# Retention, ELU block and gated block on one core: odd head pairs' outputs on the other half of the partitions, inputs in gated quarters, x stored as 2 KB rows

## The chip, the core and the metric

The kernel runs on one core of a Trainium2 chip. Its time is the device time of one execution in microseconds. Before the change the median of three runs is 872.62 us (871.51 to 873.28). The one execution that was profiled took 868.8 us, with a span of 867.0 us between its first and last instruction.

## What is computed

Three stages follow each other; all arrays are float32.

```python
# q, k, v: (4, 8, 576, 64): batch, heads, positions, head size
scores = (q @ k.T) / 8
ret = scores * D          # D[i, j] = gamma_h ** (i - j) for i >= j, else 0
x = (ret @ v) put as (2304 tokens, 512 = 8 heads * 64)
h = x @ w_in              # 512 -> 2048
y = elu(h) @ w_out        # 2048 -> 512
out = (sigmoid(y @ w_gate) * (y @ w_val)) @ w_out2    # 512 -> 1536 -> 512
```

## The kernel before, in words

**Retention** is done in 18 steps (class `Step`, `NSTEP`). A step n takes 128 positions of one batch (the last step of each half of the batches takes 64 positions of two). The eight heads are four pairs p; a pair is 128 partitions, head h = 0 on partitions 0 to 63 and h = 1 on 64 to 127. A step cuts its 128 positions into two halves X of 64. All its matmuls (L274, helper `mm`) are 64 by 64, so that one uses a quarter of TensorE's array: which half of the rows it takes is set by the partitions of what it reads, which half of the columns by the partitions of what it writes.

- `scores` (L276) fills the PSUM tile `ts`; `causal` (L283, VectorE) masks it into `a`.
- `sums` (L289) and `states` (L299) make the running state of each head in the other PSUM tile `to` and in `st`.
- `inter` (L318) multiplies the state with q: rows of half h, output (method `o`, L315) on the partitions of half h. It goes twice over pairs and heads: first with X = 1 - h, then with X = h. Steps with c = 0 (n = 0, 1, 9, 10) have a state for X = 1 only and issue half of these matmuls.
- Between its two halves `inter` puts a `nop` on SyncE (on GpSimd in step 1) that waits for the first half. `outs` (L330), which adds the part within a half (rows of half X, output on half h), starts with a wait for this `nop`. It is needed because row halves change the place that they add to.
- `x_mul` (L342, VectorE) scales the result by `cq_sb` into `xf`; `x_high` and `x_low` split it into two parts for the next matmuls, and `x_low` stores `xf` to memory (L365) in `whole[g]`, one tile [128, KB, 512] for 512 tokens, so that one step's 128 tokens are rows of 512 B.

**The feed-forward part.** `ff` is a list of units; unit s of the main loop (L1089) makes one block of 128 hidden values for 256 tokens (512 from s = 18 on): `ups` (L385, matmuls at L380), ELU, a split into `g`, and `downs` of unit s - 2 (L421, matmuls at L114 to L116). Up to s = 15 it also calls `block(s + 2)`, the retention step n = s + 2: `inter(n)`, `scores(n + 1)`, `outs(n)`, `sums(n + 1)`, then the VectorE part, the loads and the store. From s = 4 on the block stands ahead of the unit's `ups`, before that behind it. Each engine runs its instructions in the order in which they are written here.

**Loads.** All loads are issued by SyncE, in order. `Step.load` brings a step's 1 MB of q, k and v; from step 9 (`FIRST_APART`) in two parts, the second kept in the list `rest` until `begin_rest(f)` issues it behind the end of unit f's matmuls (after `ups` and after `downs`). Weights are loaded by `Weight.load` (512 KB, rows of 4 KB) and then made from 64-bit to two 32-bit parts by `Weight.chain` (ACT, VectorE, GpSimd), in a scratch tile t chosen by a number in L185. Those of w_in are `weights[0]`, `[2]`, `[4]`, `[6]` and so on; the main loop loads `weights[4]`, `[5]`, `[6]`, `[7]` and `W["i", 4]` behind the `downs` in s = 4, 7, 10, 13 and 11 (L1158). A DMA's completion is told by one of eight semaphores, which the DMAs of SyncE and ACT take in turn; a DMA that takes a semaphore whose last DMA hasn't landed waits for it on its engine.

**Later parts.** From s = 18 on the stored x is read back twice: `prep` (L1061) reads tokens 0 to 1023 in four transfers of 512 KB; `reload` (L989) reads tokens 1024 to 2047 in two of 1 MB. The rest of the ELU block and the gated block use a two by two scheme with seven products of blocks (`unit`, L518; products in the order 1, 7, 6, 2, 5, 3, 4). Converted weights are kept in memory and brought back by `restore` (L1048). In the last unit of the ELU block (`q + 1 == QN`, L1302) the gated block's first weights ("v", 0), ("g", 0) and ("s", 0) are restored.

```python
                    for n, i in zip(back[-1:] + back[:-1], (0, 2, 4, 6, 8)):
                        plan[i] = [*plan[i], lambda n=n: restore(n)]
```

Of the kernel before, what the change touches and what calls it, by code (L numbers as in the profile page):

```python
# [11 lines left out]
F32 = mybir.dt.float32  # L12
BF16 = mybir.dt.bfloat16
F32R = mybir.dt.float32r
I32 = mybir.dt.int32
# [6 lines left out]
NP = H // 2  # L22
# [6 lines left out]
HC = 64  # L29
# [25 lines left out]
def retention_elu_glu(  # L55
# [81 lines left out]
    class Weight:  # L137
        def __init__(self, src, slot, at=None, home=w_tile):
            self.src, self.slot, self.at, self.home, self.w = src, slot, at, home, None

        def load(self, raw=None):
            self.ours = raw is None
            self.raw = raw_free.popleft() if self.ours else raw
            return sp.dma_start(out=self.raw, in_=self.src.bitcast(I32))

# [36 lines left out]
    for f in range(FA):  # L182
        for n, src in (("i", w_in), ("o", w_out)):
            i = len(weights)
            W[n, f] = Weight(src[f], i % 8, (0, 0, 1, 1, 0, 1, 0, 1)[i] if i < 8 else t_slot(n, f))  # L185
            weights.append(W[n, f])
# [39 lines left out]
    class Step:  # L226
# [16 lines left out]
        def load(self):  # L243
            if self.n in SPARE:
                self.t = spare_y[SPARE[self.n]].rearrange("p (q c) -> p q c", q=NP)
            else:
                self.t = inpool.tile([128, NP, 4 * C], F32, tag="in", name="in")
            self.q, self.kT, self.k, self.v = (self.t[:, :, i * C : i * C + C] for i in range(4))
            if self.last:
                self.load_half(0)  # L250
            elif self.n < FIRST_APART:
                sp.dma_start(out=self.t, in_=ain[self.b, self.c].rearrange("p r x -> r p x"))
            else:
                self.load_pairs(0)
                rest.append(lambda: self.load_pairs(1))

        def load_pairs(self, i):
            p = slice(2 * i, 2 * i + 2)
            return sp.dma_start(out=self.t[:, p, :], in_=ain[self.b, self.c][p].rearrange("p r x -> r p x"))

# [53 lines left out]

        def o(self, h, X, p):  # L315
            return to[64 * h : 64 * h + 64, X, 256 + HC * p : 256 + HC * p + HC]

        def inter(self):  # L318

            for other in (1, 0):  # L320
                for p in range(NP):
                    for h in range(2):
                        X, r = h ^ other, slice(64 * h, 64 * h + 64)
                        if X or self.c:
                            ins = self.mm(self.o(h, X, p), self.st[X][r, p, :], self.q[r, p, HC * X : HC * X + HC], p == 0)
                if other:

                    self.swept = after((pool if self.n == 1 else sp).nop(), ins)

        def outs(self):  # L330

            for p in range(NP):
                for h in range(2):
                    for X in range(2):
                        r = slice(64 * X, 64 * X + 64)
                        ins = self.mm(self.o(h, X, p), self.v[r, p, 64 * h : 64 * h + 64], self.a[r, h, p, :],
                                      not self.c and not X and p == 0)
                        if self.swept:
                            after(ins, self.swept)
                            self.swept = None  # L340

# [18 lines left out]
        def x_low(self):  # L360
            dve.tensor_tensor(out=self.x[1], in0=self.xf, in1=self.x[0].bitcast(F32), op=ALU.subtract)
            if self.g < 4:
                if not self.at:
                    whole[self.g] = dpool.tile([128, KB, 512], F32, tag=f"x{self.g}", name="x")
                sp.dma_start(out=whole[self.g][:, :, self.at : self.at + 128], in_=self.xf)  # L365

# [435 lines left out]
    with tc.manual_schedule():  # L802
# [32 lines left out]
        for X in range(2):  # L835
            r = slice(64 * X, 64 * X + 64)
            act.dma_start(out=tri[r], in_=csmall[r, 5 * NP + 64 * X : 5 * NP + 64 * X + HC])
        act.dma_start(out=cq_sb, in_=cq)
        for X in range(2):
# [18 lines left out]

        def begin_rest(f):
            while rest:  # L860
                after(rest.pop(0)(), f.end)

        def block(n, scales=True):

            more = n + 1 < NSTEP
            steps[n].inter()
            if more:
                steps[n + 1].scores()
            steps[n].outs()
# [47 lines left out]
        warm_up(3)  # L917
        steps[1].inter()
        steps[1].outs()
# [61 lines left out]
        def close():  # L981
            raw_shut[:] = more_raws
            for r in more_raws:
                for i, o in enumerate(raw_free):
                    if o is r:
                        del raw_free[i]
                        break

        def reload(to):  # L989
            for g in (2, 3):  # L990
                to[g] = y_tile(g)
                sp.dma_start(out=to[g], in_=whole[g].rearrange("p k t -> p (k t)"))

# [67 lines left out]
        def prep():  # L1061
# [3 lines left out]

            def source(g, k):
                return whole[g][:, k * KH : k * KH + KH, :].rearrange("p k t -> p (k t)")

            def sum(name):
# [3 lines left out]
            for name, (g, k) in {"11": (0, 0), "12": (1, 0), "22": (1, 1), "21": (0, 1)}.items():  # L1073
                sp.dma_start(out=f[name], in_=source(g, k))
            for _ in range(8):
# [13 lines left out]
        for s in range(end):  # L1089
# [23 lines left out]
            if s == 0:  # L1113
                def middle():
                    stages(w2, 1)
                    steps[2].scores()
                    steps[2].sums(True)
# [13 lines left out]
            if s == 1:  # L1131
# [3 lines left out]
                warm_up(WARM[4])  # L1135
                steps[3].inter()
                steps[4].scores()
                steps[3].outs()
# [126 lines left out]
        for pair in (first, second):  # L1265
# [3 lines left out]
            for q in range(Q0, QN):  # L1269
# [19 lines left out]
                else:  # L1289
# [12 lines left out]
                    else:  # L1302
                        back += [("v", 0), ("g", 0), ("s", 0)]
                    for n, i in zip(back[-1:] + back[:-1], (0, 2, 4, 6, 8)):
                        plan[i] = [*plan[i], lambda n=n: restore(n)]
# [175 lines left out]
```

## Time and profile before

| | before |
|---|---|
| median of 3 runs | 872.62 us |
| profiled execution | 868.8 us, span 867.0 us |
| PE | 852.4 us busy, 98% |
| DVE | 664.7 us, 77% |
| ACT | 459.3 us, 53% |
| POOL | 409.4 us, 47% |
| DMA | 194.83 MB, mean 225 GB/s |
| TensorE clock | 0.997 of full speed |
| issue to landing, median: input loads of 512 KB | 5.3 us |
| w_out loads of 512 KB | 3.6 us |
| `reload`'s two loads of 1 MB | 10.5 us |

PE is TensorE's matmuls, DVE VectorE, ACT ScalarE, POOL GpSimd, SPq SyncE's queue of instructions. A busy PE counts overlapping matmuls once, so it doesn't tell how many quarters of the array work side by side; that is read from the times at which matmuls start.

### The profile page before, as it was taken

The page shows a single profiled execution, that of the slowest core. Times are in us where ns is not written, and L with a number is a line of the kernel's source. Part 1 is how long each engine was busy: PE and PEld are TensorE (multiplying, and loading weights), DVE is VectorE, ACT ScalarE, POOL GpSimd, SP SyncE. Part 2 cuts the span into 40 slices and gives each one's busy share as a digit, 9 for nine tenths or more (in the row PEclk, how much of TensorE's full clock was granted, in tenths as well). Part 3 has the DMA queues.
Part 4 walks back from the last instruction along what each step waited for, and adds up shares of the span by engine and source line. Part 5 has one row for each costly group of instructions (what it writes and reads, how often), then busy time and mean ns, then how long its engine had stood idle before and what let it go on. Part 6 is the DMA issues. An engine that isn't in the chain of part 4 may idle for free.

```text
span 867.0 us, 16196 instructions
## 1 busy us (share of the span) xinstructions
PE 852.4 (98%) x6375; PEld 728.9 (84%) x6375; DVE 664.7 (77%) x967; ACT 459.3 (53%) x833; POOL 409.4 (47%) x327
## 2 busy tenths in 40 slices
PE   8899999999999999999999999999999999999998
PEld 5798998888888888888878888888888888888886
DVE  5867758789999888887887988589967564777775
ACT  3445475677666666666665665445543344343331
POOL 2445435656546543564552565244543244334453
PEclk9999999999999999999999999999999999999999
DMA  9978628745474696898774765646574665464322
GB/s 339 298 245 245 185 74 314 292 145 202 163 229 184 230 404 227 314 377 274 274 326 176 239 239 210 218 157 196 197 277 157 229 235 194 192 237 170 112 114 98
DMA packets 63852, 194.83 MB, mean 225 GB/s; under 512 B 9888, under 2 KB 19104, under 8 KB 57376
## 3 DMA queue, kind: packets, MB, share of 16 engines
q1 hardware_dynamic: 62512, 192.30, 61.8%
q10 hardware_dynamic: 1264, 1.49, 0.5%
q8 instruction: 50, 0.82, 0.4%
q14 instruction: 26, 0.21, 0.1%
HBM read 127.19 MB, written 66.58 MB: 223 GB/s over the span
## 4 chain that ended last, share of the span: by engine, by line
PE 88%; DVE 4%; DMA 3%; issue 2%; ACT 2%; POOL 1%; SPq 0%; ACTq 0%; DVEq 0%; POOLq 0%
PE u L114 13%; PE u L115 13%; PE u L116 13%; PE acc L114 10%; PE acc L115 10%; PE acc L116 10%; PE tile L114 3%; PE tile L115 3%; PE tile L116 3%; PE to L274 3%; PE h L380 2%; DMA w<-c 2%; PE h L114 1%; PE h L115 1%; PE h L116 1%
## 5 line engine op out<-in xcount | busy, mean ns | idle before, releaser
L110 POOL TENSOR_TENSOR g<-e,g 128x512 fp32r<-128x512 f32 x95 | 133.7, 1412 | 223.8 <-ACT g L109 196.8
L114 PE MATMUL u<-x,s 128*128 128x512 f32 x288 | 112.6, 391 | 0.0
L115 PE MATMUL u<-x,s 128*128 128x512 f32 x288 | 112.3, 390 | 0.0
L116 PE MATMUL u<-x,s 128*128 128x512 f32 x288 | 112.1, 389 | 0.0
L114 PE MATMUL u<-x,w 128*128 128x512 f32 (+1 forms) x264 | 98.3, 372 | 1.5 <-DMA w<-c 1.3
L115 PE MATMUL u<-x,w 128*128 128x512 f32 (+1 forms) x264 | 98.0, 371 | 0.0
L116 PE MATMUL u<-x,w 128*128 128x512 f32 (+1 forms) x264 | 97.7, 370 | 0.0
L109 ACT CAST g<-e 128x512 fp32r<-128x512 f32 x101 | 61.9, 620 | 65.0 <-DVE e L598 39.7
L172 POOL TENSOR_TENSOR w<-t,w 128x512 fp32r<-128x512 f32 x37 | 51.0, 1378 | 41.1 <-ACT w L169 37.5
L114 PEld LDWEIGHTS u<-x,s 128*128 128x128 f32 x288 | 54.1, 188 | 11.5 <-ACT u L522 0.7
L116 PEld LDWEIGHTS u<-x,s 128*128 128x128 f32 x288 | 54.1, 188 | 11.5
L115 PEld LDWEIGHTS u<-x,s 128*128 128x128 f32 x288 | 54.2, 188 | 10.3
L759 DVE TENSOR_TENSOR y<-y,tile 128x512 f32<-128x512 f32 x76 | 51.2, 680 | 10.8 <-PE tile L116 10.6
L114 PE MATMUL acc<-g,w 128*128 128x512 f32 (+1 forms) x168 | 58.2, 346 | 0.4 <-ACT y L440 0.4
L795 DVE TENSOR_TENSOR y<-y,acc 128x512 f32<-128x512 f32 x58 | 39.1, 682 | 25.4 <-PE acc L116 25.0
L114 PEld LDWEIGHTS u<-x,w 128*128 128x128 f32 x264 | 49.8, 189 | 10.2 <-DMA w<-c 1.7
L115 PE MATMUL acc<-g,w 128*128 128x512 f32 (+1 forms) x168 | 57.7, 344 | 0.0
L116 PE MATMUL acc<-g,w 128*128 128x512 f32 (+1 forms) x168 | 57.7, 343 | 0.0
L116 PEld LDWEIGHTS u<-x,w 128*128 128x128 f32 x264 | 49.7, 188 | 8.7
L115 PEld LDWEIGHTS u<-x,w 128*128 128x128 f32 x264 | 49.9, 189 | 7.4
L675 DVE TENSOR_TENSOR y<-y,acc 128x512 f32<-128x512 f32 (+1 forms) x68 | 39.6, 606 | 19.8 <-PE acc L116 17.9
L114 PE MATMUL acc<-w,g 128*128 128x512 f32 (+1 forms) x152 | 54.1, 356 | 0.0
(226 smaller groups left out, 2418.3 us busy)
## 6 DMA issues: line engine op xcount, KB each, us to landing
w<-c SPq DMA_DIRECT2D x72, 512.0 KB, 6.7
c<-w SPq DMA_DIRECT2D x48, 512.0 KB, 4.9
s<-c SPq DMA_DIRECT2D x22, 1024.0 KB, 7.1
c<-s SPq DMA_DIRECT2D x18, 1024.0 KB, 4.9
y<-y SPq DMA_DIRECT2D x8, 1024.0 KB, 6.2
in<-in_ain SPq DMA_DIRECT2D x6, 1024.0 KB, 8.9
raw<-in_w_in SPq DMA_DIRECT2D x12, 512.0 KB, 4.8
in<-in_ain SPq DMA_DIRECT2D x12, 512.0 KB, 5.3
```

Of the source, the lines that this page charges most:

```text
L109: act.copy(hi, src)
L110: lo_engine.tensor_tensor(out=lo, in0=src, in1=hi.bitcast(F32), op=ALU.subtract)
L114: pe.matmul(out_, wh, xh, start=start, stop=False, skip_group_check=shared)
L115: pe.matmul(out_, wh, xl, start=False, stop=False, skip_group_check=shared)
L116: return pe.matmul(out_, wl, xh, start=False, stop=stop, skip_group_check=shared)
L172: lo_engine.tensor_tensor(out=w[:, 1, :], in0=f, in1=w[:, 0, :].bitcast(F32), op=ALU.subtract)
L274: return pe.matmul(out_, w, x, start=start, stop=True, skip_group_check=True)
L380: self.end = pe.matmul(h, w[:, a, c[k]], x[:, b, k, t], start=i + k == 0, stop=i == 2 and k == KB - 1)
L675: dve.tensor_tensor(out=out_, in0=out_, in1=a, op=ALU.add)
L759: dve.tensor_tensor(out=y, in0=y, in1=a, op=ALU.add)
L795: dve.tensor_tensor(out=o, in0=o, in1=a, op=ALU.add)
```

## The change

- `o` puts the outputs of pairs 1 and 3 on the other half of the partitions, so x has the two heads of these pairs in each other's place. `cq_sb` and the rows of w_in are loaded to match: each of these loads becomes three, one of 128 partitions and two of 64.
- The first half of `inter` now adds with all four quarters. The wait for the `nop` stands ahead of `inter`'s second half, and `scores` of the next step between the two. The `nop` of step 0 goes to GpSimd.
- From step 9 on inputs come in four transfers of 256 KB, one pair each. `begin_rest` issues one, in three places: behind the `nop`, after `ups`, after `downs`.
- `whole[g]` is [128, 4, KB, 128]: a step's store has rows of 2 KB. Its readers fetch each of the KB blocks by itself, in pieces of 512 B (256 KB a transfer).
- `weights[6]` uses scratch tile 1 in place of 0. The last unit of the ELU block restores v0, s0, o, o, g0 at places 0, 1, 3, 5, 7.

```diff
         def load(self, raw=None):
...
+            if self.turned:
+                to_, src = (a.rearrange("p (k two x) -> p k two x", k=KB // 2, two=2) for a in (self.raw, self.src.bitcast(I32)))
+                load = sp.dma_start(out=to_[:, :, 0], in_=src[:, :, 0])
+                for i in range(2):
+                    sp.dma_start(out=to_[64 * i : 64 * i + 64, :, 1], in_=src[64 - 64 * i : 128 - 64 * i, :, 1])
+                return load
...
-            W[n, f] = Weight(src[f], i % 8, (0, 0, 1, 1, 0, 1, 0, 1)[i] if i < 8 else t_slot(n, f))
+            W[n, f] = Weight(src[f], i % 8, (0, 0, 1, 1, 0, 1, 1, 1)[i] if i < 8 else t_slot(n, f))
+            W[n, f].turned = n == "i"
...
-                self.load_pairs(0)
-                rest.append(lambda: self.load_pairs(1))
...
+                self.load_pair(0)
+                rest.extend(lambda p=p: self.load_pair(p) for p in range(1, NP))
+
+        def load_pair(self, p):
+            return sp.dma_start(out=self.t[:, p, :], in_=ain[self.b, self.c][p])
...
         def o(self, h, X, p):
+            h ^= p % 2
             return to[64 * h : 64 * h + 64, X, 256 + HC * p : 256 + HC * p + HC]
 
-        def inter(self):
+        def sweep(self, ins):
+            if self.swept:
+                after(ins, self.swept)
+                self.swept = None
+
+        def inter(self, between=None):
...
-                            ins = self.mm(self.o(h, X, p), self.st[X][r, p, :], self.q[r, p, HC * X : HC * X + HC], p == 0)
+                            ins = self.mm(self.o(h, X, p), self.st[X][r, p, :], self.q[r, p, HC * X : HC * X + HC], other == 1 and p < 2)
+                            self.sweep(ins)
                 if other:
 
-                    self.swept = after((pool if self.n == 1 else sp).nop(), ins)
+                    self.swept = after((pool if self.n < 2 else sp).nop(), ins)
+                    begin_rest()
+                    if between:
+                        between()
...
-                    whole[self.g] = dpool.tile([128, KB, 512], F32, tag=f"x{self.g}", name="x")
-                sp.dma_start(out=whole[self.g][:, :, self.at : self.at + 128], in_=self.xf)
+                    whole[self.g] = dpool.tile([128, 4, KB, 128], F32, tag=f"x{self.g}", name="x")
+                sp.dma_start(out=whole[self.g][:, self.at // 128], in_=self.xf)
...
-        act.dma_start(out=cq_sb, in_=cq)
+        pairs_of = lambda a: a.rearrange("d (a two) i -> d a two i", two=2)
+        act.dma_start(out=pairs_of(cq_sb)[:, :, 0], in_=pairs_of(cq)[:, :, 0])
+        for i in range(2):
+            act.dma_start(out=pairs_of(cq_sb)[64 * i : 64 * i + 64, :, 1], in_=pairs_of(cq)[64 - 64 * i : 128 - 64 * i, :, 1])
...
-        def begin_rest(f):
-            while rest:
-                after(rest.pop(0)(), f.end)
+        def begin_rest(f=None):
+            if rest:
+                load = rest.pop(0)()
+                if f:
+                    after(load, f.end)
...
-            steps[n].inter()
-            if more:
-                steps[n + 1].scores()
+            steps[n].inter(steps[n + 1].scores if more else None)
             steps[n].outs()
...
+        def fetch_x(out_, g, ks):
+            for i, k in enumerate(ks):
+                sp.dma_start(out=out_[:, i * 512 : i * 512 + 512].rearrange("p (a t) -> p a t", a=4), in_=whole[g][:, :, k, :])
+
         def reload(to):
             for g in (2, 3):
                 to[g] = y_tile(g)
-                sp.dma_start(out=to[g], in_=whole[g].rearrange("p k t -> p (k t)"))
+                fetch_x(to[g], g, range(KB))
...
             for name, (g, k) in {"11": (0, 0), "12": (1, 0), "22": (1, 1), "21": (0, 1)}.items():
-                sp.dma_start(out=f[name], in_=source(g, k))
+                fetch_x(f[name], g, range(k * KH, k * KH + KH))
...
-                    for n, i in zip(back[-1:] + back[:-1], (0, 2, 4, 6, 8)):
+                    if q + 1 < QN:
+                        back, places = back[-1:] + back[:-1], (0, 2, 4, 6, 8)
+                    else:
+                        back, places = [back[i] for i in (2, 4, 0, 1, 3)], (0, 1, 3, 5, 7)
+                    for n, i in zip(back, places):
                         plan[i] = [*plan[i], lambda n=n: restore(n)]
```

## Rows read from the trace of the kernel before

**Rows 1.** Waits of PE behind 110 us: who for whom, total, times, longest.
```profile
PE u L114 <- DMA w<-c: 1.3, 1, 1.3
PE u L114 <- DVE u L542: 0.2, 1, 0.2
```
**Rows 2.** Busy us of PE, PEld, DVE, ACT, POOL; clock, DMA share, GB/s.
```profile
20.00:40.00 20.00, 16.46 (x493) 13.72 (x493) 16.99 (x31) 8.20 (x18) 6.75 (x7) 1.00 0.91 304
40.00:60.00 20.00, 20.00 (x561) 19.05 (x560) 11.51 (x21) 9.81 (x25) 10.66 (x11) 1.00 0.95 299
```
**Rows 3.** PE in order of time, step 11: start us, us, instruction.
```profile
73.61 0.28 PE L116 MATMUL acc<-g,w 128*128 128x256 f32 x1
73.82 0.27 PE L274 MATMUL to<-in,y 64*64 64x64 f32 x1
...
74.69 0.27 PE L274 MATMUL ts<-in 64*64 64x64 f32 x1
...
75.21 0.22 PE L274 MATMUL to<-a,in 64*64 64x64 f32 x1
...
75.67 0.22 PE L274 MATMUL to<-in 64*64 64x64 f32 x1
```
**Rows 4.** PE in order of time, step 9, which has c = 0.
```profile
62.78 0.79 PE L274 MATMUL to<-y,y 64*64 64x64 f32 x13
...
63.35 0.28 PE L274 MATMUL ts<-in 64*64 64x64 f32 x3
```
**Rows 5.** SyncE's DMA issues: start us, us of issuing, count last.
```profile
52.29 0.34 SPq L144 DMA_DIRECT2D raw<-in_w_in  x1
...
93.67 0.66 SPq L266 DMA_DIRECT2D in<-in_ain  x1
...
434.53 0.93 SPq L1055 DMA_DIRECT2D w<-c  x2
```
**Rows 6.** Step 0's gate: SyncE's issue, then PE behind the nop (L328).
```profile
10.18 0.53 SPq L144 DMA_DIRECT2D y<-in_w_out  x1
...
10.83 0.69 PE L274 MATMUL to<-a,in 64*64 64x64 f32 x32 [0.19 <-SPq L328]
```
**Rows 7.** Start of the kernel: a wait of SyncE's queue.
```profile
SPq L252 <- DMA small<-in_csmall: 2.9, 1, 2.9
```
**Rows 8.** Start of the kernel: a piece of the chain that ended last.
```profile
2.44 6.00 DMA cq_sb<-in_cq
```
**Rows 9.** Start of the kernel, in order of time.
```profile
4.66 0.38 SPq L252 DMA_DIRECT2D in<-in_ain  x1
...
7.69 0.68 ACT L154 ACTIVATE t<-raw 128x512 f32<-128x512 f32 x1 [1.99 <-DMA raw<-in_w_in]
...
11.82 1.05 POOL L271 TENSOR_TENSOR in<-in,small 128x512 f32<-128x512 f32 x1 [1.39 <-DMA in<-in_ain]
...
12.20 1.22 DVE L161 CUSTOM_DVE_ANT_0 t<-raw,t 128x1024 uint16<-128x1024 uint16 x1
```
**Rows 10.** Stretches with one x store (512 B), then one weight load (4 KB).
```profile
102.00:105.00 3.00, 3.00 (x84) 2.87 (x86) 1.14 (x3) 2.46 (x5) 1.86 (x3) 1.00 0.42 109
105.00:108.20 3.20, 2.79 (x58) 2.52 (x48) 3.13 (x7) 1.50 (x5) 0.73 (x1) 1.00 0.40 148
```
**Rows 11.** Around the second reading of x: issue, two VectorE sums, PE's product 4.
```profile
292.06 1.60 SPq L992 DMA_DIRECT2D y<-x  x2
...
304.48 1.22 DVE L472 TENSOR_TENSOR y<-y 128x1024 f32<-128x1024 f32 x1
305.62 0.69 DVE L542 TENSOR_TENSOR u<-e,u 128x512 f32<-128x512 f32 x1
...
307.50 0.39 PE L114 MATMUL u<-x,w 128*128 128x512 f32 x1
```
**Rows 12.** VectorE behind the first reading of x.
```profile
150.04 1.22 DVE L1071 TENSOR_TENSOR fs<-fg,fs 128x1024 f32<-128x1024 f32 x1
153.54 0.69 DVE L397 SCALAR_TENSOR_TENSOR e<-e,h 128x512 f32<-128x512 f32 x1 [2.27 <-ACT e L394]
```

More of the change, by code (lines that the diff above doesn't have):

```diff
@@ L139, in __init__ @@
             self.src, self.slot, self.at, self.home, self.w = src, slot, at, home, None
+            self.turned = False
         def load(self, raw=None):
@@ L253, in load @@
             else:
-                self.load_pairs(0)
-                rest.append(lambda: self.load_pairs(1))
-        def load_pairs(self, i):
-            p = slice(2 * i, 2 * i + 2)
-            return sp.dma_start(out=self.t[:, p, :], in_=ain[self.b, self.c][p].rearrange("p r x -> r p x"))
+                self.load_pair(0)
+                rest.extend(lambda p=p: self.load_pair(p) for p in range(1, NP))
+        def load_pair(self, p):
+            return sp.dma_start(out=self.t[:, p, :], in_=ain[self.b, self.c][p])
         def load_half(self, X):
@@ L337, in outs @@
                                       not self.c and not X and p == 0)
-                        if self.swept:
-                            after(ins, self.swept)
-                            self.swept = None
+                        self.sweep(ins)
         def x_mul(self):
@@ L917, in retention_elu_glu @@
         warm_up(3)
-        steps[1].inter()
+        steps[1].inter(steps[2].scores)
         steps[1].outs()
@@ L1064, in prep @@
             f = {"11": fa, "t2": fa, "12": fb, "t3": fb, "t1": fb, "22": fc, "21": fd, "t4": fd}
-            def source(g, k):
-                return whole[g][:, k * KH : k * KH + KH, :].rearrange("p k t -> p (k t)")
             def sum(name):
@@ L1115, in middle @@
                     stages(w2, 1)
-                    steps[2].scores()
                     steps[2].sums(True)
@@ L1135, in retention_elu_glu @@
                 warm_up(WARM[4])
-                steps[3].inter()
-                steps[4].scores()
+                steps[3].inter(steps[4].scores)
                 steps[3].outs()
```

## The prediction, made before the change was run

> **What bounds the kernel now.** I read the busy shares first: TensorE is busy 98% of the span. Next I asked where it waits. Behind 110 us it waits 1.5 us in all, 1.3 of them once, for a restored weight [rows 1]. So from 110 us to the end a microsecond that TensorE saves or loses is one of the span, and what happens earlier counts by how much sooner or later TensorE gets there. Third, the stretches ahead of that. From 20 to 40 us TensorE is idle 3.5 us, VectorE is busy 17.0 of 20 and the DMA engines 0.91 of the time: the start is bound by a chain of loads and VectorE work. From 40 us, where the retention steps lie between feed-forward units, TensorE is busy all the time [rows 2]. Last, its order of time in one step. In step 11 `inter`'s 32 matmuls (each of its 16 is two passes) take from 73.82 to 74.69 us, 0.87 us; `outs`, with as many passes, takes from 75.21 to 75.67, 0.46 us [rows 3]. The difference is that `outs` uses four quarters of the array at a time and `inter` two. In a busy stretch that is real work time that can be saved, though the page shows PE as busy in both.
>
> **Four quarters.** With odd pairs on the other half, four successive matmuls of a half of `inter` have four different quarters, as in `outs`. A full `inter` goes from 0.87 to 0.46 us: 0.41 saved [rows 3]. Of steps 4 to 17 twelve are full: 4.9 us. Steps 9 and 10 have half the work; today it takes from 62.78 to 63.35, 0.57 us [rows 4], and two quarters in place of one should halve it: 0.28 each, 0.6. Steps 0 to 2 lie under VectorE's chain and save nothing at TensorE's end; step 3 I count at 0.4, since its `outs` feed the next VectorE step. Sum: 5.9 us. The lower bound of the saving is nothing, if the second pair of quarters didn't run beside the first; `outs`, which has all four, speaks against it.
>
> **The gate.** What is new is where TensorE waits. Today `inter`'s second half follows at once, and `scores` too, so SyncE has 0.9 us behind the first half's end to run its `nop` before `outs` begin. Afterwards the second half waits, with only `scores` as cover, 75.21 - 74.69 = 0.5 us [rows 3]. Everything in the rest of the step stands behind this wait: the second half, `outs`, `sums`, the unit's `ups`, and through them VectorE and ACT. TensorE would want the second half 0.23 + 0.47 = 0.70 us behind the start of `inter`. The `nop` itself needs the end of the first half (about 0.23 + 0.25 us) and a way there and back; step 0 shows the way back: SyncE ends an issue at 10.71 and TensorE goes on at 10.83, 0.12 us [rows 6]. That just fits. So the gate costs nothing when SyncE is free, and what SyncE is doing decides. In a usual step one more quarter of an input is issued behind the `downs`, whose end is 73.61 + 0.28 = 73.89, 0.07 us behind the start of `inter`: with 0.35 us of issuing it still fits. Where a weight load stands there as well it doesn't. A w_in load is issued in 0.34 us [rows 5]; afterwards it is three issues. A second issue at once costs 0.93 / 2 = 0.46 us, and one of 64 partitions took 0.66 us [rows 5]. So one load goes from 0.34 to between 3 x 0.34 = 1.0 and 0.34 + 2 x 0.66 = 1.7 us; I take 1.3 (0.34 + 2 x 0.46), nearest to back-to-back issues. Main loop s = 4 and 11: 0.07 + 0.08 (TensorE's end seen by SyncE, an estimate from the 0.12) + 0.46 (quarter) + 1.3 + 0.12 = 2.0 us behind the start of `inter`, 1.3 later than wanted. s = 10 has no quarter there: 0.9. s = 7, a w_out load of one issue: 0.4. Step 17 has no `scores` as cover: 0.3. Sum of the gates: 1.3 + 1.3 + 0.9 + 0.4 + 0.3 = 4.2 us, between 3.0 and 5.5 by the two prices of an issue. There is one more wait: the last quarter of step 13 and of step 16 goes out in the step ahead of its use, some 5 us before `scores` need it, and input loads of 512 KB take 5.3 us to land (the table above); I count 0.2 each. So the steady part gains 5.9 - 4.6 = 1.3 us.
>
> **The start.** SyncE's second input load is issued at 4.66, and before that it waits 2.9 us for the first small load [rows 7, 9]: eight completion semaphores in turn, and this is the ninth DMA. Afterwards `cq` is three DMAs and the first w_in load three, so this input is the thirteenth and waits not for the first small load but for about the fifth DMA, a part of `cq`. `cq` is issued at 2.44 and lands at 8.44 [rows 8]. So the input goes out at some 8.4 in place of 4.66. It doesn't land 3.8 us later, for today its bytes queue behind others: it lands at 11.82 [rows 9], and 1 MB at the 304 GB/s of rows 2 takes 3.4 us, so 8.4 + 2 + 3.4 = 13.8, 2.0 later (the 2 us are an estimate of what passes before bytes flow: a w_out load of 512 KB lands in 3.6 us by the table, of which its bytes take 1.7 at 304 GB/s). The last third of the first w_in load must wait for a landing too, of about the fourth DMA, which like `cq` comes near 8 us, and is there at 10 to 10.5 in place of 7.69 [rows 9]. Both feed the VectorE chain that runs without a gap from 12.20 on [rows 9] through the stretch of rows 2. I take 2.2 us later for everything behind; bounds are 0.5 us (if the pieces land as fast as they are issued) and 3.1 (if the w_in thirds and `cq` keep the old latency of 6 us). Nothing gives this back: later than that TensorE sets the pace.
>
> **The order of restores.** The 1.3 us wait of rows 1 is for ("v", 0), the first weight of the gated block: its issue is the first of the pair at 434.53 [rows 5], though its slot has long been free. At place 0 of that unit it goes out some 6 us earlier. The wait goes: 1.3 us. Late next is ("g", 0), which moves behind, but only product 4, the last of the unit, reads it. Bounds: 0 to 1.3.
>
> **Rows of 512 B.** The stores get cheaper, but nobody waits for them. The readings get dearer. 256 KB of x in 512 B pieces and a little more took 0.42 x 3.0 = 1.26 us of all DMA engines, at 109 / 0.42 = 260 GB/s; 4 KB rows went at 148 / 0.40 = 370 GB/s [rows 10]. The second reading, 2 MB, then takes 8.1 in place of 5.7 us. VectorE's sum of it starts at 304.48, and behind it in VectorE's order stands the sum at 305.62 that frees the bank of product 4 at 307.50 [rows 11]. Landing was just ahead of 304.48 (issued from 292.06 on, with a median of 10.5 us by the table); at 306.6 or so the second sum ends at 306.6 + 1.2 + 0.7 = 308.5, and TensorE waits 1.0 us. The first reading is used at 150.04; 3 to 5 us later eats the 2.27 us that VectorE waits anyway and some of the distance of two units between ELU and `downs` [rows 12], so I count nothing. Sum 0.7 (between 0 and 4). The Trainium skill, "DMA: Bandwidth & Descriptors", section "Specifications", puts the least size for line rate at 512 B; by that these readings would cost nothing and the sum below would be 0.7 us lower. Rows 10 speak against it.
>
> Scratch tile 1 for `weights[6]` frees ACT of a wait that TensorE hardly feels: 0.
>
> **Sum.** -5.9 (quarters) + 4.2 (gates) + 0.4 (late quarters of inputs) + 2.2 (start) - 1.3 (restores) + 0.7 (readings) = +0.3 us. The profiled execution of 868.8 us (867.0 and 1.8 around it) would become 869.1. The median of the runs shown is 3.8 us above the profiled one; I put the change on the median: 872.62 + 0.3, rounded 873.0.
>
> **Rivals.** (1) *The steps win*: SyncE's short issues overlap with what TensorE does anyway, the gates cost 1.5 us and the start 1. Then -5.9 + 1.5 + 0.4 + 1.0 - 1.3 + 0.3 = -4.0: 868.6 us. For it: TensorE is the only engine at its limit from 40 us on [rows 2]. Against it: issues on SyncE are in order, and the `nop` is one of them. (2) *Slower, by the late readings*: pieces of 512 B are read in a stretch in which the DMA engines have no room, and VectorE, in order, holds everything behind the first sum. It decides from a landing at 305.6 us on: each microsecond past that is one of TensorE's. With 4 us at the second reading, and the rest as above, +3.6 to +4: 876.5 us. For it: VectorE's next instruction is wanted within 1.2 us [rows 11]. Against it: 260 GB/s is not half of 370. (3) *The pace of `inter` doesn't change*: then the sum is +6.2 and 878.8; `outs` in rows 3 speaks against it.
>
> **How the numbers follow.** The forecast, no change that can be told, has a chance of 0.36; rival 1 0.34; rival 2 with a dear start 0.27; rival 3 0.03. A difference below 0.2% (1.7 us) can't be told from none here. Faster 0.34, same 0.36, slower 0.30. The forecast's own range is 871 to 874.8; since cases of both signs hold most of the chance, the range for 8 in 10 reaches into both, 867.6 to 877.
>
> **What would show it.** Right: `inter`'s halves of some 0.23 us each; TensorE waiting for L328 in the steps behind s = 4, 10 and 11 and hardly elsewhere; the second input issued near 8.4 us and everything behind it some 2 us later; no wait of TensorE for a restored weight. Wrong: no wait for L328 above 0.5 us, a start as early as today, or a long wait of VectorE at its sums of x.

## The result: slower by 1%, and the profile after

The changed kernel takes 880.22 us (median of 5 runs, 879.7 to 881.9), the kernel before on the same chip 872.62 us (871.51 to 873.88). The ratio is 1.0097, with a 95% interval from 1.0078 to 1.0117: slower. The forecast was 873.0 us in a range of 867.6 to 877, so the time lies outside it. The profiled execution took 881.9 us, its span 880.0. That is 13.0 us over the span before, while the medians differ by 7.6 (the ratio makes it 8.5): the execution that was profiled before lies 3.8 us below its median, the one after 1.7 above its own.

Where the time comes from is read best from when TensorE begins each unit's `ups`. I took the starts of some units from both timelines:

```
unit s            0       4       9      12      13      17
before us     18.64   49.09   76.30   94.38  100.47  116.67
after us      23.99   54.52   82.72  103.53  111.68  127.70
later by       5.35    5.43    6.42    9.15   11.21   11.03
```

There are three lumps: 5.35 us before the first unit, 2.7 us from s = 9 to 12, and 2.1 us from 12 to 13. The steps in between were to have given 5.9 us back, and gave back almost nothing.

The first lump, in order of time at the start of the changed kernel (start us, us, engine, line, instruction; in brackets the idle time before it and what ended it); it answers to [rows 8, 9]:

```profile
0.73 0.44 SPq L260 DMA_DIRECT2D in<-in_ain  x1
...
4.81 0.69 SPq L147 DMA_DIRECT2D raw<-in_w_in  x1
...
6.99 1.21 SPq L149 DMA_DIRECT2D raw<-in_w_in  x2
...
8.24 0.59 SPq L260 DMA_DIRECT2D in<-in_ain  x1
...
10.72 1.28 ACT L161 ACT_TABLE_LOAD   x1 [10.72 <-DMA raw<-in_w_in]
...
12.01 0.66 ACT L161 ACTIVATE t<-raw 128x512 f32<-128x512 f32 x1
...
13.51 0.42 DVE L319 TENSOR_TENSOR st<-y,to 128x256 f32<-128x256 f32 x1 [5.41 <-ACT y L317]
...
13.98 1.18 PE L281 MATMUL to<-in,y 64*64 64x64 f32 x10 [5.44 <-DVE st L319]
```

The second input goes out at 8.24 us, where the forecast had 8.4. But it isn't held by a landing of its own, a part of `cq`, as forecast. It stands in SyncE's order behind the parts of the first w_in load, and those are held (SyncE's waits up to 12 us):

```profile
SPq L147 <- DMA small<-in_csmall: 3.6, 1, 3.6
SPq L149 <- DMA tri<-in_csmall: 1.5, 1, 1.5
```

So all three parts go out late, at 4.81 and from 6.99 on, where the one load before went out at 1.23, and the last part lands only at about 10.7. Then comes something that I had not seen as a step at all: ACT's table load, 1.28 us, now stands behind the wait for that weight. The kernel before had it in time that ACT spent waiting anyway:

```profile
4.42 1.28 ACT L154 ACT_TABLE_LOAD   x1 [4.42 <-issue]
```

So ACT's first work begins at 12.01 instead of 7.69, and step 0's `inter` waits 5.44 us for a state that ACT and VectorE make behind it.

What TensorE waits for between 12 and 110 us (total, times, longest):

```profile
PE to L281 <- DVE st L319: 5.7, 2, 5.4
PE to L281 <- SPq L342: 4.9, 4, 1.6
PE to L281 <- issue: 4.2, 4, 1.3
PE ts L281 <- DMA in<-in_ain: 1.9, 1, 1.9
```

The second row is the gate (L342 is the `nop`, L328 before). Its waits behind s = 10 and 11, 1.19 and 1.57 us, are the second lump; the two behind s = 4 and 7, 1.58 and 0.57 us, lie where the delay grows by 1.0 us. The fourth row is a late quarter of an input, the third lump. The third row has no releaser; more on it below. One gate, in the step behind s = 11, answers to [rows 3]:

```profile
99.71 0.46 PE L281 MATMUL to<-y,y 64*64 64x64 f32 x16
99.99 0.65 PE L281 MATMUL ts<-in 64*64 64x64 f32 x32
100.23 0.56 SPq L147 DMA_DIRECT2D raw<-in_w_in  x1
...
100.84 1.25 SPq L149 DMA_DIRECT2D raw<-in_w_in  x2
...
102.20 0.46 PE L281 MATMUL to<-y,y 64*64 64x64 f32 x16 [1.57 <-SPq L342]
...
102.49 0.65 PE L281 MATMUL to<-a,y 64*64 64x64 f32 x32
```

A half of `inter` takes 99.99 - 99.71 = 0.28 us and the other 0.29: the quarters do run beside each other. But SyncE is in three issues of a weight load until 102.09, and only then runs the `nop`.

Behind s = 12 the late quarter costs more than its wait. TensorE's granted clock there (stretch, its length, TensorE's busy us, clock, DMA share, GB/s):

```profile
108.00:110.00 2.00, 0.65 (x43) 1.00 0.38 109
110.00:112.00 2.00, 1.77 (x61) 0.66 0.07 19
112.00:114.00 2.00, 2.00 (x11) 0.50 0.31 120
114.00:116.00 2.00, 2.00 (x27) 0.99 0.03 11
```

TensorE waits 1.94 us until 109.35, and from about 111 to 114 us it then runs at half clock, 1.2 in place of 2.4 GHz. The kernel before has the full clock in [rows 10].

Behind 110 us the waits answer to [rows 1]:

```profile
PE tile L115 <- POOL g L110: 1.5, 1, 1.5
PE acc L114 <- DVE y L457: 0.4, 1, 0.4
PE tile L114 <- DVE y L774: 0.3, 1, 0.3
```

The 1.3 us for a restored weight are gone, as forecast. A wait of 1.5 us for GpSimd, some 5 us further on, has taken their place.

### The profile page after: what moved, and what is told of

It is laid out like the page before. It is cut to its first block, busy times and chain, and to the rows that moved or that the text cites. A ratio compares the mean times of both kernels' runs of the same rounds, so it can differ in the third digit from the quotient of the medians.

```text
span 880.0 us, 16304 instructions
## 1 busy us (share of the span) xinstructions
PE 849.1 (96%) x6370; PEld 724.0 (82%) x6375; DVE 665.2 (76%) x967; ACT 460.4 (52%) x833; POOL 409.7 (47%) x327
## 4 chain that ended last, share of the span: by engine, by line
PE 80%; DVE 6%; DMA 4%; ACT 3%; issue 3%; SPq 2%; POOL 1%; ACTq 0%; POOLq 0%; DVEq 0%
PE u L114 13%; PE u L115 13%; PE u L116 13%; PE acc L114 9%; PE acc L116 9%; PE acc L115 9%; PE tile L114 3%; PE tile L115 3%; PE tile L116 3%; PE to L281 2%; PE h L395 2%; DMA raw<-in_w_in 1%; SPq L1009 1%; DMA fg<-x 1%; ACT x L491 1%
```

## The experiments

Each kernel was timed in five rounds beside the kernel before on the same chip. The ratio is that of the two.

**Weights and `cq` turned ahead of the launch.** The rows of w_in and `cq` are exchanged in the host's layout, so that each is one transfer again; all else of the change stays.

```diff
-            W[n, f].turned = n == "i"
+            W[n, f].turned = False
...
-        act.dma_start(out=pairs_of(cq_sb)[:, :, 0], in_=pairs_of(cq)[:, :, 0])
-        for i in range(2):
-            act.dma_start(out=pairs_of(cq_sb)[64 * i : 64 * i + 64, :, 1], ...)
+        act.dma_start(out=cq_sb, in_=cq)
...
+    cq[:, :, :, 1] = half[::-1, :, :, 1]
...
+        out[:fs, :, :, :, 1] = w[:fs, ::-1, :, :, 1]
```

> The changed kernel with the rows of w_in and of cq exchanged in the host's layout, so that each of these loads is one transfer again. Theory (the three-part loads cost the start 5.4 us and hold the gate in the steps behind w_in loads, 1.58 + 1.19 + 1.57 us): the first feed-forward matmul is back from 23.99 to about 18.6 us, the three long waits for the nop go, the time is 880.2 - 5.4 - 4.3 = 870.5 us. Rival (the gate costs what TensorE's way to SyncE and back costs, whatever is loaded): only the start comes back, 874.8 us, and the waits for the nop stay.

872.29 us, ratio 1.0008 [0.9993, 1.0023]. The loss is gone, and of waits for the `nop` none of 0.4 us or more is left. Its start: second input at 4.97, table load at 4.43, first unit at 20.06 us. That is the larger part of the answer, but it is no gain: nearly 2 us more than my theory had.

```profile
4.43 1.28 ACT L161 ACT_TABLE_LOAD   x1 [4.43 <-issue]
4.97 0.38 SPq L260 DMA_DIRECT2D in<-in_ain  x1
```

**Only the start of it.** `cq` and the first two w_in blocks are turned by the host, the later w_in loads stay in three parts (`turned = n == "i" and f > 1`).

> The changed kernel with only cq and the first two w_in blocks in the host's layout: the start has one transfer for each again, the later w_in loads stay in three. Theory: first feed-forward matmul at about 18.6 us, the waits for the nop stay at some 4.9 us in all, 880.2 - 5.4 = 874.8 us. Rival (the late start is taken up again further on, where loads and VectorE have room): under 2 us of it reach the end, 878 to 880 us.

876.96 us, 1.0054 [1.0033, 1.0075]; the waits at the gate are still there, 4.3 us in three. Together the three runs split the loss in ratios to before: start 1.0097 - 1.0054 = 0.0043 (3.7 us), weight loads at the gates 1.0054 - 1.0008 = 0.0046 (4.0 us), all the rest 0.0008 (0.7 us); each of the first two can be off by some 2.5 us, by the intervals.

**The weight load behind the gate.** Still three transfers, but issued behind the next step's `nop` instead of in front of it.

```diff
+                    while late:
+                        late.pop(0)()
...
-                load = w.load()
+                late.append(w.load)
```

> The changed kernel with the weight loads of the main loop issued behind the next step's nop in place of ahead of it; they stay in three transfers. Theory (what holds the gate is SyncE's time of issuing ahead of the nop): the waits for the nop fall from 4.9 us to under 0.6, and the time by 4.3 us to 875.9. Rival (the three transfers make the DMA engines late, whichever place they have): the time stays within 1 us of 880.2.

877.08 us, 1.0069 [1.0045, 1.0092], about one us more than expected. The gate's waits go from 4.9 us to

```profile
PE to L281 <- SPq L342: 1.5, 3, 0.7
```

so it is the place of the issues on SyncE's queue, not the transfers, that TensorE waits for.

**The kernel before with the start in three parts.** `cq` and the first two w_in loads are three transfers each, with no rows exchanged and nothing else changed.

```diff
+            if any(self is w for w in weights[:3:2]):
...
+                load = sp.dma_start(out=to_[:, :, 0], in_=src[:, :, 0])
+                for i in range(2):
+                    sp.dma_start(out=to_[64 * i : 64 * i + 64, :, 1], in_=src[64 * i : 64 * i + 64, :, 1])
```

> The kernel before with cq and the first two w_in loads in three transfers of the same bytes, rows not exchanged, and nothing else of the change. Theory (eight completion semaphores in turn: six more transfers at the start make later ones wait for landings, and ACT's table load comes to stand behind the wait): first feed-forward matmul from 18.64 to about 24 us, time 872.6 + 5.4 = 878.0 us. Rival (the late start of the changed kernel comes from its retention steps or from the exchanged rows): no change, 872.6 us.

877.63 us, 1.0067 [1.0046, 1.0088]: 5.8 us from the start alone, in a kernel that has nothing else of the change. Its first unit begins at 25.59 us, later still than in the changed kernel. The same rows stand in its trace:

```profile
8.17 0.59 SPq L258 DMA_DIRECT2D in<-in_ain  x1
...
10.43 1.28 ACT L160 ACT_TABLE_LOAD   x1 [10.43 <-DMA raw<-in_w_in]
...
13.69 1.60 PE L280 MATMUL to<-in,y 64*64 64x64 f32 x16 [5.15 <-DVE st L318]
```

So the start is settled. What was open then was why the rest, with quarters that run and a restored weight that isn't waited for, gains nothing. The next three take one part each out of the first experiment's kernel.

**Steps 13 and 16 loaded whole** (`elif self.n < FIRST_APART or self.n in (13, 16)`).

> The host-turned kernel (872.3 us) with the inputs of steps 13 and 16 loaded whole in place of in quarters. Theory (step 16's last quarter is issued too late, TensorE waits 1.99 us for it and its clock falls behind it): that wait goes and the time falls by 2 to 3 us to about 870. Rival (the wait only moves on to VectorE's or GpSimd's work for the same step): within 1 us of 872.3.

871.07 us, 1.0009 [0.9997, 1.0020]. The wait of 2.0 us for the late quarter, and the half clock behind it, are gone from the trace, and the profiled span is 867.0 against 872.0. The ratio is the same, to within some 1.7 us by the intervals. The wait is no accident of one execution: it stands, with 1.1 to 2.9 us, in all six profiled kernels that load step 16 in quarters. Why the time doesn't fall without it stays open.

**Step 2's scores at their old place** (`steps[1].inter()` with the scores behind step 1's work).

> The host-turned kernel (872.3 us) with step 2's scores back behind the first feed-forward matmuls. Theory (these scores ahead of step 1's outs make the first feed-forward matmul 1.4 us late, 20.06 in place of 18.64): it comes back to below 19 us and the time falls by 1 to 1.5 us to about 871. Rival (the lateness is VectorE's, slowed beside GpSimd): no change, 20 us and 872.3.

873.14 us, 1.0040 [1.0025, 1.0055]: no gain, rather a loss; my theory of this one falls.

**x stored and read as before.**

```diff
-                    whole[self.g] = dpool.tile([128, 4, KB, 128], F32, tag=f"x{self.g}", name="x")
+                    whole[self.g] = dpool.tile([128, KB, 512], F32, tag=f"x{self.g}", name="x")
```

> The host-turned kernel (872.3 us) with x stored and read as before (512 B rows written, 4 and 8 KB rows read). Theory (reading in 512 B pieces makes both readings late by some microseconds and costs TensorE 1 to 1.5 us): 871 us, and VectorE no longer waits for the second reading. Rival (the cheaper 2 KB stores help the retention steps as much): no change.

871.24 us, 1.0010 [0.9996, 1.0023]: no difference that can be told.

**The quarters alone.** The kernel before with the outputs of odd pairs on the other half (rows turned by the host), the first half gated, `scores` between the halves. Inputs in halves, x, restores and step 2's scores as before.

```diff
+            h ^= p % 2
...
-                            ins = self.mm(self.o(h, X, p), ..., p == 0)
+                            ins = self.mm(self.o(h, X, p), ..., other == 1 and p < 2)
+                            self.sweep(ins)
...
-            steps[n].inter()
-            if more:
-                steps[n + 1].scores()
+            steps[n].inter(steps[n + 1].scores if more else None)
```

> The kernel before with the quarters alone: outputs of odd pairs on the other half (w_in and cq turned by the host), the wait ahead of the second half of inter, scores of the next step between; input halves, x rows, restores and step 2's scores as before. Theory (each inter saves 0.41 us in a stretch that TensorE bounds, and the gate is free where SyncE has nothing to issue): 4 to 5.5 us less than the kernel before, some 867 us. Rival (TensorE gives the saving back in waits of its own in the same steps, those that the profile calls issue, and in the gate): within 1.5 us of the kernel before, 871 to 873 us.

872.87 us, 1.0022 [1.0007, 1.0038]. The rival of the expectation came nearer, and this is the finding that turns the question: the part that was to gain 5.9 us gains nothing by itself. Yet a step in which TensorE doesn't wait is shorter: from s = 8 to 9 and from 11 to 12 5.09 us in place of 5.55, from 13 to 14 4.79 in place of 5.07. The time goes in "issue" waits, 6.6 us between 12 and 110 us against 2.6 before. Two of them in order of time:

```profile
30.95 0.29 PE L274 MATMUL to<-y,y 64*64 64x64 f32 x1 [1.74 <-issue]
...
82.88 0.65 PE L274 MATMUL to<-in 64*64 64x64 f32 x31
86.22 0.36 PE L274 MATMUL to<-in 64*64 64x64 f32 x1 [2.69 <-issue]
```

The second one stands between the 31st and the 32nd pass of the same `sums`: no semaphore can lie there. And behind it the clock (columns as above):

```profile
84.00:87.00 3.00, 0.78 (x3) 0.78 0.67 170
87.00:90.00 3.00, 3.00 (x16) 0.50 0.33 98
90.00:93.00 3.00, 3.00 (x66) 0.58 0.00 0
93.00:96.00 3.00, 3.00 (x103) 1.00 0.72 212
```

That unit takes 7.68 us in place of 5.54. The first wait has the same behind it: half clock from 31.07 to 37.89 us. The execution profiled before has the full clock from 15.24 us to its last 2 us. The waits stand at the same instruction in kernel after kernel: the kernel before has 1.19 us at 83.10, in the same `sums`.

**The same with a longer stream.** If the waits hang on a place in TensorE's instruction stream, they must move when instructions are put in ahead of them, where TensorE has time. Some of the first twelve warm-up matmuls are split in four:

```diff
-            pe.matmul(h, warm[:, :128], warm, start=True, stop=True)
+            for c in range(4 if i < fours else 1):
+                c = slice(128 * c, 128 * c + 128) if i < fours else slice(0, 512)
+                pe.matmul(h[:, c], warm[:, :128], warm[:, c], start=True, stop=True)
...
-        warm_up(WARM[0])
+        warm_up(WARM[0], 4)
```

> The kernel before with the quarters alone (outputs of odd pairs on the other half, host-turned inputs, first half gated), and 12 more matmuls in TensorE's stream: four of the first twelve warm-up matmuls are split into four of 128 columns each, at a place where TensorE waits anyway. Theory: the three long issue waits of the quarters alone (1.74 us in step 3's inter, 2.69 us in step 12's sums, 1.46 us near 105 us) hang on the place in TensorE's instruction stream, and with the half clock behind the first of them they eat the quarters' gain. Then they move to 12 matmuls earlier (the first into the warm-up that waits for VectorE anyway) or shrink, the way from the second to the third unit of the feed-forward falls from 15.1 us to about 12, and the time to 867 to 869. Rival: they belong to the order of the work (a dependency that the profile does not show): they stay at the same instructions, and the time stays within 1 us of 872.9.

869.75 us, 0.9983 [0.9970, 0.9996]. The first wait has moved by 12 exactly: from 9 passes into step 3's `inter` to behind the first of four warm-ups, 3 + 9 passes earlier. In order of time:

```profile
27.89 0.82 PE L124 MATMUL h<-y 128*128 128x512 bf16 x3 [1.29 <-issue]
...
31.21 0.68 PE L276 MATMUL to<-y 64*64 64x64 f32 x28 [0.94 <-DVE e L356]
33.87 0.33 PE L276 MATMUL to<-y 64*64 64x64 f32 x4 [1.98 <-issue]
```

From this wait to the next are 3 + 32 + 32 + 32 + 28 = 127 passes (the rest of the warm-up, `inter`, `scores`, `outs`, and 28 of the 32 of `sums`). But the way from the second to the third unit, which I had expected to fall to 12 us, takes 14.76: the next place has brought its own wait.

**The control, and two shifts forecast to the pass.** The kernel before with the same 12 more; then the quarters alone with 24 and with 36 more.

> The kernel before with the same 12 more matmuls and nothing else, the control. Theory: its own issue waits (0.92 us at 34 us, 1.19 us at 83 us) move or change by a few tenths, and the time stays within 2 us of the 870.5 to 871.8 of before, in either direction. Rival: the issue waits stay where they are and the time is the same within 0.5 us.

870.56 us, 0.9996 [0.9982, 1.0011]. Its waits moved (1.15 us at the same warm-up, 1.77 at the same pass of `sums`; the 1.19 of step 12 fell to 0.16), the time didn't.

> The quarters alone once more, with eight of the first warm-up matmuls split into four, so that TensorE's stream is 24 matmuls longer ahead of the retention steps (12 in the run before). Theory (the issue waits come at fixed places of the stream, 128 matmul passes apart, and show where a burst of short passes reaches such a place too early): the wait that stood 9 passes into step 3's inter without the shift, and behind the first of the four warm-up matmuls with 12, stands now behind 21 of the 32 passes of step 3's sums ahead of them, and the next one behind 16 of the 32 passes of step 4's sums; they are 1 to 2 us each where they show, and the time lies between 867.5 and 872. Rival (they belong to the work): a wait of over 0.5 us stands at step 3's inter or at the warm-up ahead of it.

870.09 us, 0.9989 [0.9977, 1.0002]:

```profile
25.41 0.56 PE L276 MATMUL to<-y 64*64 64x64 f32 x21 [0.19 <-POOL y L273]
26.84 0.45 PE L276 MATMUL to<-y 64*64 64x64 f32 x11 [0.86 <-issue]
...
32.08 0.46 PE L276 MATMUL to<-y 64*64 64x64 f32 x16 [1.60 <-DVE e L356]
32.93 0.46 PE L276 MATMUL to<-y 64*64 64x64 f32 x16 [0.39 <-issue]
```

> The same with all twelve first warm-up matmuls split, 36 more. Theory: the places are 36 passes earlier than without the shift: behind 9 of the 32 passes of step 3's sums, and behind 4 of the 32 of step 4's sums. No wait of over 0.3 us stands at step 3's inter. The time lies between 867.5 and 872, by how much of the waits falls into waits that are there anyway. Rival: as above.

869.63 us, 0.9982 [0.9969, 0.9996]:

```profile
26.57 0.38 PE L276 MATMUL to<-y 64*64 64x64 f32 x9 [0.19 <-POOL y L273]
27.95 0.57 PE L276 MATMUL to<-y 64*64 64x64 f32 x23 [1.00 <-issue]
...
33.34 0.33 PE L276 MATMUL to<-y 64*64 64x64 f32 x4 [1.60 <-DVE e L356]
34.04 0.68 PE L276 MATMUL to<-y 64*64 64x64 f32 x28 [0.36 <-issue]
```

Behind 21 and 16 passes, then behind 9 and 4, as calculated ahead: the place belongs to the stream, not to the work. Only their size was off: 0.4 to 1.0 us, where I had expected 1 to 2.

**What ends these waits** can be read from the DMA packets in the traces. Queue q8 brings instructions, in packets of 16,384 bytes. The quarters alone, from 83.5 to 84.0 us (the queue, its packets, MB, share):

```profile
q8 instruction: 1, 0.02, 11.7%
```

TensorE had stopped at 83.53. This packet begins at 83.84 and lands at 84.77, and TensorE goes on at 86.22. It is so everywhere: between 12 and 110 us the 17 traces of this case have 57 waits of TensorE of 0.5 us or more without a releaser, and each ends 1.1 to 1.7 us after such a packet landed. Counted in TensorE's weight loads from the start, they stand at eleven places alone, one list for all kernels: the 479th, 606th, 734th, 862nd, 990th, 1244th, 1371st, 1755th, 1883rd, 2011th and 2267th, all of them one, two or three times 127 or 128 apart. The shifts left these places where they are and moved the work under them.

**The restores alone**, in the kernel before.

> The kernel before with the new order of the restores alone. Theory (from the trace of the changed kernel: the wait for the restored weight is gone and one of 1.5 us for GpSimd's low part of g stands 5 us behind it): no gain, within 0.7 us of before; the wait of 1.3 us for the restored weight is gone and a wait for GpSimd's g of 1.3 to 1.7 us near 448 us has taken its place. Rival (the prediction): 1.3 us faster.

870.91 us, 0.9994 [0.9981, 1.0008]. The only wait over 0.15 us behind 110 us is now

```profile
PE tile L115 <- POOL g L110: 1.6, 1, 1.6
```

The profiled execution of this kernel is of use beyond that. What it changes lies behind 400 us, so in the stretches below it is the kernel before, and it has

```profile
31.18 0.27 PE L274 MATMUL to<-y,y 64*64 64x64 f32 x1 [1.11 <-issue]
...
87.72 0.27 PE L274 MATMUL to<-in 64*64 64x64 f32 x1 [2.24 <-issue]
```

in a span of 871.4 us, where the execution profiled before had its first one a packet later, 0.92 us, and 1.19 at the second place, in 867.0. So these waits differ from one execution to the next, and the packets tell by what: at the second place the packet began 1.32 us before TensorE stopped in the execution with 1.19 us, 0.21 before in the one with 2.24, and 0.31 us after it stopped where the quarters alone wait 2.69.

**The change mended**: host-turned, steps 13 and 16 whole, x as before; and the same with 12 more matmuls.

> The whole change with its three counts against it taken out together: weights and the cq tile turned in the host's layout, so that each is one transfer; steps 13 and 16 loaded whole; x stored and read as before. Theory (the quarters' gain is real, 4 to 5 us, and is given back by issue waits): 869 to 871.5, no more than 1.5 us from before. Rival (what is left of the loss lay in the readings and in the late quarters): 866 to 868.

869.83 us, 0.9990 [0.9977, 1.0002].

> The same, with the 12 more matmuls of the control in the first warm-up. Theory: the issue wait in step 3's inter (1.3 to 1.5 us with the half clock behind it) moves into a wait that is there anyway, and the time falls to 866 to 868.5. Rival: it stays, and the time is within 1 us of the unshifted one.

870.06 us, 1.0000 [0.9984, 1.0015]; here the shift gave nothing, against my theory. Of all kernels only the quarters alone with 12 or 36 more matmuls beat the kernel before by more than the interval, by 0.17% and 0.18%: 1.5 us of the 5.9.

## Why the prediction was wrong, step by step

**The start: mis-sized, 2.2 us forecast, 5.35 in the trace, 3.7 to 5.8 by the runs.** That more transfers make later ones wait for landings was right. That the second input came at 8.24 us against 8.4 was partly luck: I had it wait for a part of `cq`, and it only stood behind the three w_in parts, which wait for `small` and `tri`. Of the three I had held up only the last. I let the last third of the first w_in load arrive at "10 to 10.5"; it came at 10.7. What my chain lacked is the table load. [rows 9] show ACT's first instruction at 7.69 with 1.99 us of waiting in front of it, and I did not ask what ACT had done in that time. The 1.28 us then stand right on the chain, and with 10.72 + 1.28 = 12.0 in place of 7.69 the first state is 4.3 us late, not 2.2. My upper bound, 3.1, came from two landings and had no instruction in it.

**The gates: right.** 4.2 us forecast, 4.9 in the trace (1.58, 0.57, 1.19, 1.57 against 1.3, 0.4, 0.9, 1.3, and nothing at step 17), 4.0 by the runs. Three issues took 0.56 + 1.25 and a little between them, 1.86 us, not 1.3: a little more than by the upper price of [rows 5], 1.7. (By the two prices the bounds of this term come out at 3.3 and 5.4, not 3.0 and 5.5.)

**The quarters: the step that failed.** The forecast was 5.9 us off the span. The pace was about right: halves of 0.28 us instead of 0.23, full steps shorter by 0.28 to 0.46. But I counted each tenth as one of the span because TensorE is busy from 40 us on [rows 2]. The quarters alone took 1.9 us more, with its stream moved 1.5 less. Rival 3 of the prediction, 878.8 us, came nearest by its number, but not by its reason: the pace did change. What took the place of the gain is a limit that the busy share hides: TensorE's instructions. The page of the changed kernel says it in two places (TensorE's passes and weight loads; the queue, its packets, MB, share):

```profile
PE 849.1 (96%) x6370; PEld 724.0 (82%) x6375; DVE 665.2 (76%) x967; ACT 460.4 (52%) x833; POOL 409.7 (47%) x327
...
q8 instruction: 50, 0.82, 0.4%
```

0.82 MB in 50 packets is 16.4 KB a packet, and 6370 + 6375 instructions in 50 packets are 255 each: 128 passes with their weight loads. That is the distance of the waits, and each of the longer waits ends behind the landing of one of these packets. A step has 32 passes each of `inter`, `scores`, `outs` and `sums`, 128 short ones in some 2 us, so the burst of one step uses up a whole packet. Faster quarters use it up sooner: the 128 passes ahead of the 1883rd weight load took 2.7 us before and 2.3 with the quarters alone, and the packet that TensorE then waited for began 1.6 and 2.7 us after the first of them. No run changed how the packets come, and what sets when one begins stays open.

Between 12 and 110 us such waits are 6.6 us in the quarters alone, 4.7 to 6.1 in the three shifted kernels and 2.6 in the execution profiled before. Behind some of them the clock falls to half: behind the 1.98 us of the run with 12 more it was 0.73 and then 0.70 in the next two stretches of 3 us, behind 2.46 us at 78.97 in the run with 24 more it stayed at full. What the shifts give the quarters alone, 2.9 to 3.5 us by the ratios, goes with this clock. Between 20 and 110 us the quarters alone had 13.7 us at half clock, each of the three shifted kernels 3.4. Over all timed executions the median of the mean granted clock is 0.992 for the quarters alone, 0.996, 0.9965 and 0.9975 with 12, 24 and 36 more, and 0.998 for the kernel before beside each. Taken as TensorE's loss, (1 - clock) of the time, that is 7.0 us against 3.5, 3.0 and 2.2, and 1.7 before. These are upper bounds, since TensorE has not work at every moment: the kernel before with 12 more has 0.996 too, and its time is the same. Why the mended change gains nothing by the shift stays open.

**The late quarters: 0.4 forecast.** In the trace one wait of 1.94 us, with half clock behind it, 2.1 us between s = 12 and 13. Loading these steps whole takes it out of the trace and leaves the ratio where it was (1.0009 against 1.0008).

**The restores: 1.3 us forecast, nothing gained** (0.9994 alone). I looked at what is late next among the weights, ("g", 0), and not among the other things that the next products need. The row was there to be found: GpSimd's low part of g is made by an engine that is behind, and TensorE, no longer held up by the weight, comes 1.3 us earlier to wait for it.

**The readings: the wait was there, its price was too high.** The working gave 1.0 us, and the sum took 0.7 without a reason. VectorE's sum of the second reading does wait, 1.27 us, but TensorE waits only 0.17 us for VectorE behind it, at 319.93. Its two longer waits for VectorE, 0.37 us at 171.5 and 0.34 at 362.0, lie elsewhere; that they make 0.7 is chance. With x as before the time is the same within the interval. Rival 2, 876.5 us by a late reading, had the sign but not the cause.

**The base.** The trace that I worked from was a lucky one, 3.8 us below its median, with few of the waits without releaser: 2.6 us, where the execution of the restores alone has 3.9. I put the change on the median, but read the price of "issue" from the lucky execution, where it is 2.6 us, and left it out.

## What to carry to other kernels

A transfer that is split in three costs little in bytes and much in places: count what each more issue holds up on its queue, what waits for an earlier landing because of it, and which one-time work of the engine behind (here ACT's table load) loses its cover. A busy engine is not a bound until one has asked what feeds it, its instructions too: before a saving in short matmuls is counted, look for waits with no releaser in the middle of a burst, whether they stand a fixed number of passes apart, and whether a packet of instructions lands just ahead of their end. And a wait that goes is worth only the distance to whatever is late next on any engine, not only in the same queue.

## What was not expected of the hardware

TensorE stops without a releaser at fixed places of its stream, 127 or 128 passes apart (16.4 KB of instructions a packet), for 0.2 to 2.7 us. All 57 such waits of 0.5 us or more end 1.1 to 1.7 us behind the landing of an instruction packet, and the longest are those whose packet began last, counted from TensorE's stop. When the stream is lengthened by 12, 24 or 36 matmuls they come that many passes earlier in the work. Behind a wait of 1.94 us the granted clock was at half for some 3.4 us and behind one of 2.69 us for nearly 7 (worked out from the two tables of the clock above, a stretch's length times (1 - clock) / 0.5), most of it with TensorE at work again; a unit of 5.5 us then took 7.7. A table load of ACT, 1.28 us, runs ahead of the first activation's wait in one kernel (4.42 us) and behind it in another (10.72), with the same activation on ACT. What differs are the loads ahead of it, three transfers for one, and ACT's own last issue, which ends at 4.39 us in the one and at 7.11 in the other. Why that moves it, no run shows.
